# Attention and a feed-forward block on one core: weights' rounding with longer lags, second product started without sums of g, transposes in the score banks, first q and k loaded ahead of the branch

## Chip, core and metric

The kernel runs on one core of one Trainium2 chip. The metric is the device time of one execution in microseconds (us). TensorE is called PE here, its weight loads PEld, VectorE DVE, ScalarE ACT, GpSimd POOL; SP is SyncE, whose queue issues every DMA of this kernel.

## What is computed

```python
# q, k, v: (8, 12, 448, 64); g_q, g_k: (64,); w_in: (768, 2048); w_out: (2048, 768)
q_n, k_n = rmsnorm(q, g_q), rmsnorm(k, g_k)       # x / sqrt(mean(x*x) + 1e-6) * g
scores = q_n @ k_n.T / sqrt(64)
attn = softmax(scores)
x = (attn @ v) laid out as (8 * 448, 12 * 64)      # 3584 tokens, 768 columns
h = x @ w_in
out = relu(h) ** 2 @ w_out                         # (3584, 768)
```

q, k and v are float32; the two weights come as float64, and the kernel makes float32 of them from their 32-bit halves.

## The kernel before

**Spans and pairs.** A branch at the start (L928) picks the version whose scores need no row maximum; that is the one that runs. Its eight batches are four *spans* of two batches. A span has 12 attention *pairs* (two heads of one batch), then a first product (x by w_in) and a second product (g by w_out). Both products use a scheme with seven block products in place of eight: sums of quarters of x (xC, L642 to L654) and of g (gC, `combine`, L691 to L702) are the moving operands, sums of quarters of the weights the stationary ones. The seven sums of a weight block (A11, S2, S1, S3, A12, A22, S4) are made once, stored in DRAM (w1s, w2s) and loaded again in every span (`load_blocks`, L533, five buffers of tag sw).

**Rounding of the weights** (`prepare`, L438 to L510) is a generator of 35 *ticks* with four steps each; a tick t works on weight unit t and on the two or three units before it. Per unit: DVE takes the exponent out (L486), ACT bends it twice (L492, L493), DVE adds the sign (L471), cuts the mantissa (L476) and joins it (L477), ACT scales it (L483), POOL multiplies two halves (L459); for every second unit POOL makes four sums (L466) and SP stores the seven blocks (L499, L502). Loads of the raw words (L433, L436) go to one of five places (`place_of`), three of them towards the end. `EARLY`, `LATE` and `ALL` (L837) say how many steps are taken in which stage of span 0: 48 during its 12 attention pairs, 72 between its 56 first products, 20 between the two *alone* pairs that follow.

**Order.** There is no scheduler: the order on each engine is the program's. Span 0: 12 pairs alone, first product with rounding, two pairs of span 1 alone, `combine` for all of g (L871), then the second product of span 0 with the other ten pairs of span 1 threaded into it (L887 to L890). Spans 1 and 2: first product, then second product with the next span's 12 pairs (the *mixed* stage). Span 3: first and second product.

**A pair** (`attention`, L656): scores of key chunks 0 and 1 (L604, exponent on ACT at L607), `norm` of pair i+2 (ACT square, DVE reduction, POOL power L576 and two multiplications L578), in a mixed stage a stretch of second product, then the transposes of pair i+1 (L590; ACT copies them out at L596), scores of chunks 2 and 3, the values (L621), the sums of the exponents (L632), reciprocal and product on DVE (L638, L639). In `first_product` a helper `ahead` (L842) does the norms, loads and transposes of the next span's first pairs.

**PSUM.** Pool ps_s has two buffers of two banks (scores; pa of the first product), ps_o one bank each for values and sums, ps_m two single banks. ps_m serves pb, pc and pd, the accumulators ps of the second product, the two transposed tiles pt, and po, in which `deliver` (L776) turns a finished block for the output; ACT copies po out (L781). A tile waits until the one that held its buffer has been read.

The loop around the second product, which the change rewrites:

```python
for m in range(HC):                    # HC = 3
    for i in uses2:                    # A11, A12, S2, S1, S3, A22, S4
        ps = ps_m.tile(...)
        for c in range(HF): ...        # HF = 8 matmuls, a yield behind each
        ...                            # DVE adds; then, if a block is done, deliver() and a yield
```

Of the kernel before, what the change touches and what calls it, by code (L numbers as in the profile page):

```python
# [302 lines left out]

@with_exitstack
def attention_then_ffn_bounded(
# [9 lines left out]
    out: bass.AP,  # L315
):
# [28 lines left out]
    P = 128  # L345
# [22 lines left out]
    mhalf = consts.tile([SP, 2 * 2 * NJ], F32, name="mhalf")  # L368
    gT = consts.tile([P, NFC, 2 * S], F32, name="gT")
# [18 lines left out]
    WORDS, BLOCKS, LAST = 5, 3, 25  # L388
# [13 lines left out]
    def place_of(n):  # L402

        return n % WORDS if n < LAST else (0, 3, 4)[(n - LAST) % 3]
# [33 lines left out]
    def prepare(t):  # L438
# [24 lines left out]
        def total(n, dst, x, y, op):  # L463
            if there(n) and n % 2:
                b = parts(n)[0]
                nc.gpsimd.tensor_tensor(b[dst], b[x], b[y], op)  # L466

        if there(t - 1) and doubles:

            b, e, eu, low, f, high = parts(t - 1)  # L470
            nc.vector.scalar_tensor_tensor(eu, high, 0x80000000, eu, ALU.bitwise_and, ALU.bitwise_or)  # L471
        if there(t - 2):
            value(t - 2, 0)
        yield
        if there(t - 1) and doubles:
            nc.vector.tensor_scalar(high, high, 0xFFFFF, None, ALU.bitwise_and)  # L476
# [3 lines left out]
        total(t - 2, S1, A21, A22, ALU.add)  # L480
        yield
        if there(t - 1) and doubles:
            nc.scalar.activation(f, f, AF.Copy, bias=1.0, scale=2.0 ** -20)  # L483
        if there(t) and doubles:
            b, e, eu, low, f, high = parts(t)
            nc.vector.tensor_scalar(eu, high, 20, 0x7FF, ALU.logical_shift_right, ALU.bitwise_and)  # L486
        total(t - 2, S2, S1, A11, ALU.subtract)
        total(t - 2, S3, A11, A21, ALU.subtract)
        yield
        if there(t) and doubles:  # L490

            nc.scalar.activation(e, eu, AF.Relu, bias=clamp1, scale=-1.0)  # L492
            nc.scalar.activation(eu, e, AF.Relu, bias=clamp2, scale=-(2.0 ** 23))  # L493
        total(t - 2, S4, A12, S2, ALU.subtract)
# [34 lines left out]
    uses2 = (A11, A12, S2, S1, S3, A22, S4)  # L529
# [3 lines left out]
    def load_blocks(upto):  # L533

        while len(stream) < min(upto, NSPAN * (N1 + N2)):
# [7 lines left out]
            else:  # L543
                n -= N1
                src = w2s[n // (7 * (HF // 4)), uses2[n // (HF // 4) % 7], n % (HF // 4)]
# [7 lines left out]
    def load(i):  # L553
        b, h0 = i // NPAIR, 2 * (i % NPAIR)
        qk = loads.tile([SP, 2, 2, NJ * D], F32, tag="qk", name="qk")
        for dst, src in ((qk[:, 0], q), (qk[:, 1], k)):
            nc.sync.dma_start(dst, src[b, h0:h0 + 2].rearrange("h (p j) d -> p h (j d)", j=NJ))
        qks[i] = qk
# [26 lines left out]
    def transposes(i):  # L585
        qkn = normed.pop(i)
        pts[i] = [ps_m.tile([P, S], F32, tag="m", name="pt") for _ in range(2)]
# [10 lines left out]
    def scores(work, i, c, pe_sums):  # L598
# [7 lines left out]
        pr = work.tile([SP, 2, S], F32, tag="pr", name="pr", bufs=5)  # L606
# [49 lines left out]
    def attention(work, first, end, alone):  # L656
# [3 lines left out]
        for i in range(first, end):  # L660
# [12 lines left out]
            if i + 1 < last:  # L673
                transposes(i + 1)
                if not alone:
                    take_transposes(i + 1)
# [10 lines left out]
            if not alone:  # L687
                yield
# [77 lines left out]
    def second_product(work, span):  # L766
# [9 lines left out]
        def deliver(ct, col, t):  # L776
            pt = ps_m.tile([P, 512], F32, tag="m", name="po")
# [6 lines left out]
        for m in range(HC):  # L784
            for i in uses2:
                ps = ps_m.tile([P, S], F32, tag="m", name="ps")
                for c in range(HF):
                    load_blocks(n + 5)
                    nc.tensor.matmul(ps, stream[n][:, c % 4], rhs_of[i][:, c], start=c == 0, stop=c == HF - 1)  # L789
                    n += c % 4 == 3  # L790
                    if c < HF - 1:
                        yield
# [49 lines left out]
    def ahead(u, nxt):  # L842
# [4 lines left out]
        if u == 7 * (HF - 2):  # L847
            norm(nxt + 1)
# [114 lines left out]
```

## Time and profile before

| | us |
|---|---|
| median of 3 runs | 1643.68 (1640.68 to 1644.63) |
| the profiled execution, its own time | 1645.17 |
| its span, first to last instruction | 1643.4 |
| PE busy | 1515.0 (92%) |
| DVE, POOL, ACT busy | 727.7, 519.3, 484.7 |
| mean granted clock of PE, share of full speed | 0.977 |

The time of a run is the span and 1.8 us around it. "Busy" of PE counts the modelled length of overlapping matmuls; the distance from the start of one to the start of the next tells more, and stage lengths tell most. The kernel's float32 matmul is two instructions in the trace: 768 + 576 rows of ps are 672 matmuls of the program.

### The profile page before, as it was taken

To read this page: it belongs to the slowest core of one execution; us is meant where nothing else is said; L and a number is where in the kernel's file an instruction comes from. 1 tells how busy PE (TensorE), PEld (TensorE's weight loads), DVE (VectorE), ACT (ScalarE), POOL (GpSimd) and SP (SyncE) were. 2 spreads that over 40 slices of the span, in tenths; PEclk is the share of its full clock that TensorE was granted. 3 is DMA by queue.
4 is the path that set the end of the run, shared out by engine and by line. 5 is a ranking of instruction groups with operands and counts; after the bars stand their busy time and mean duration, and the time that the engine had idled before them with its cause. 6 is when DMAs were issued, how large, how long until landed. Compare 5 with 4: busy or idle time off the path is not lost.

```text
span 1643.4 us, 14375 instructions
## 1 busy us (share of the span) xinstructions
PE 1515.0 (92%) x5160; PEld 710.4 (43%) x5160; DVE 727.7 (44%) x849; ACT 484.7 (29%) x669; POOL 519.3 (32%) x391
## 2 busy tenths in 40 slices
PE   6999897747999999999999999989999999999998
PEld 2433443313444445444444445544444445555544
DVE  3787766456444422335445442334445551332001
ACT  4775554522232202113333311113332221111000
POOL 4795678652222002333223101242222200221000
PEclk9999998878999999999999999999999999999999
DMA  4565774641323232232332323223322223223332
GB/s 150 176 192 186 263 270 155 202 146 55 96 78 97 72 92 87 74 104 80 97 96 81 92 67 94 87 83 98 88 83 85 72 62 94 88 87 92 103 105 63
DMA packets 157716, 180.36 MB, mean 110 GB/s; under 512 B 10692, under 2 KB 134084, under 8 KB 157636
## 3 DMA queue, kind: packets, MB, share of 16 engines
q1 hardware_dynamic: 157636, 179.35, 36.3%
q8 instruction: 43, 0.70, 0.2%
q14 instruction: 37, 0.30, 0.1%
HBM read 146.28 MB, written 33.03 MB: 109 GB/s over the span
## 4 chain that ended last, share of the span: by engine, by line
PE 77%; DVE 7%; POOL 6%; ACT 4%; issue 4%; DMA 2%; SPq 1%; POOLq 0%; DVEq 0%; ACTq 0%
PE ps L789 31%; PE sc L604 9%; PE pav L621 7%; PE pd L713 7%; PE pc L713 7%; PE pa L713 6%; PE tot L632 4%; PE pb L713 3%; PE pt L590 2%; POOL gC L459 2%; POOL gC L466 1%; POOL rstd L576 1%; DVE acc L612 1%; ACT qkT L596 1%; POOL qkn L578 1%
## 5 line engine op out<-in xcount | busy, mean ns | idle before, releaser
L789 PE MATMUL ps<-gT,sw 128*128 128x448 f32 x768 | 310.9, 553 | 20.3 <-DMA sw<-w2s 10.8
L576 POOL TENSOR_TENSOR rstd<-rstd,mhalf 112x16 f32<-112x16 f32 x48 | 150.0, 3126 | 443.7 <-DVE rstd L575 420.6
L721 POOL TENSOR_TENSOR gT<-gT 128x448 f32<-128x448 f32 x112 | 112.7, 1007 | 519.6 <-ACT gT L717 519.6
L607 ACT ACTIVATE pr<-sc 112x896 f32<-112x896 f32 x192 | 166.0, 914 | 260.2 <-PE sc L604 260.1
L789 PE MATMUL ps<-gC,sw 128*128 128x448 f32 x576 | 230.1, 546 | 4.1 <-ACT osb L781 2.7
L789 PEld LDWEIGHTS ps<-gT,sw 128*128 128x128 f32 x768 | 142.7, 192 | 173.2 <-issue 143.8
L604 PE MATMUL sc<-qkT 64*112 64x448 f32 x768 | 175.7, 577 | 12.7 <-ACT pr L607 12.0
L638 DVE RECIPROCAL rec<-tot 128x448 f32<-128x448 f32 x48 | 142.0, 2958 | 78.2 <-PE tot L632 78.1
L621 PE MATMUL pav<-pr,vt 112*64 112x448 f32 x768 | 163.7, 550 | 3.4 <-DVE xT L639 3.4
L789 PEld LDWEIGHTS ps<-gC,sw 128*128 128x128 f32 x576 | 106.2, 190 | 118.0 <-issue 111.0
L713 PE MATMUL pa<-xT,sw 128*128 128x448 f32 x384 | 154.9, 539 | 0.0
L717 ACT ACTIVATE gT<-gT 128x448 f32<-128x448 f32 x96 | 55.3, 576 | 316.7 <-DVE gT L747 189.0
L612 DVE TENSOR_TENSOR acc<-acc,pr 112x896 f32<-112x896 f32 x68 | 78.8, 1159 | 140.7 <-ACT pr L607 137.1
L578 POOL TENSOR_TENSOR qkn<-qk,rstd 112x512 f32<-112x512 f32 x96 | 104.8, 1113 | 3.8
L781 ACT COPY osb<-po 112x512 f32<-112x512 f32 x48 | 28.2, 587 | 257.2 <-PE po L779 257.1
L713 PEld LDWEIGHTS pa<-xT,sw 128*128 128x128 f32 x384 | 72.9, 191 | 71.1 <-issue 71.1
L604 PEld LDWEIGHTS sc<-qkT 64*112 64x112 f32 x768 | 62.6, 177 | 93.6 <-issue 64.5
L596 ACT ACTIVATE qkT<-pt,gains 128x448 f32<-128x448 f32 x96 | 58.8, 636 | 131.7 <-PE pt L590 131.7
L621 PEld LDWEIGHTS pav<-pr,vt 112*64 112x64 f32 x768 | 51.2, 138 | 104.7 <-issue 80.1
L612 DVE TENSOR_TENSOR acc<-pr 112x896 f32<-112x896 f32 x34 | 37.1, 1092 | 131.5 <-ACT pr L607 131.5
L713 PE MATMUL pd<-xT,sw 128*128 128x448 f32 x192 | 81.7, 564 | 12.9 <-DVE z L736 12.9
L713 PE MATMUL pd<-xC,sw 128*128 128x448 f32 x192 | 82.5, 568 | 11.6 <-DMA sw<-w1s 11.1
(78 smaller groups left out, 1516.4 us busy)
## 6 DMA issues: line engine op xcount, KB each, us to landing
sw<-w1s SPq DMA_DIRECT2D x224, 192.0 KB, 2.4
sw<-w2s SPq DMA_DIRECT2D x168, 256.0 KB, 2.7
qk<-in_q_dram SPq DMA_DIRECT2D x48, 224.0 KB, 3.2
qk<-in_k_dram SPq DMA_DIRECT2D x48, 224.0 KB, 3.6
vt<-in_v_dram SPq DMA_DIRECT2D x48, 224.0 KB, 3.1
w1s<-gC SPq DMA_DIRECT2D x8, 1344.0 KB, 5.8
w2s<-gC SPq DMA_DIRECT2D x24, 448.0 KB, 4.4
out_dram<-osb SPq DMA_DIRECT2D x48, 224.0 KB, 2.9
```

The lines of the kernel that those rows point to most:

```text
L576: nc.gpsimd.tensor_tensor(rflat, rflat, mhalf, ALU.pow)
L578: nc.gpsimd.tensor_tensor(qkn[:, s].rearrange("p j h d -> p h j d"), qk[:, s].rearrange("p h (j d) -> p h j d", d=D), rstd[:, s].rearrange ...
L596: nc.scalar.activation(qkTs[i][:, s], pt, AF.Copy, scale=gains[:, s:s + 1])
L604: nc.tensor.matmul(sc[:, h, 0:S], qkT[rows, 1, c * SP:(c + 1) * SP], qkT[rows, 0, :], start=True, stop=True)
L607: nc.scalar.activation(pr, sc[:, :, 0:S], AF.Exp)
L612: nc.vector.tensor_tensor(accs[i], probs[i, 0] if c == 1 else accs[i], pr, ALU.add)
L621: nc.tensor.matmul(pavs[i][h * D:(h + 1) * D, :], vs[i][:, h, c, :], pr[:, h, :], start=(c == 0), stop=(c == NJ - 1))
L632: nc.tensor.matmul(tots[i][h * D:(h + 1) * D, :], ones, pr[:, h, :], start=first, stop=last)
L638: nc.vector.reciprocal(rec, tots.pop(i))
L713: nc.tensor.matmul(ps, stream[n][:, c], rhs[:, c], start=first and c == 0, stop=c == HC - 1, skip_group_check=not first)
L721: nc.gpsimd.tensor_tensor(g, g, g, ALU.mult)
L789: nc.tensor.matmul(ps, stream[n][:, c % 4], rhs_of[i][:, c], start=c == 0, stop=c == HF - 1)
```

## The change

- Load of the first pair's q and k (`load_pair`) and a small Exp on ACT stand ahead of the branch. q and k have two fixed buffers, qk0 and qk1.
- The rounding's steps are put in another order with longer lags: each consumer on another engine stands a step or more later, the four sums a tick later; from tick 12 on, S1 and S3 are made on DVE. There are six places for raw words (four towards the end), `LATE` is 33 ticks in place of 30: 84 steps in the first product, 8 in the alone pairs. pr has four buffers in place of five.
- The second product takes A11 and A12 of all three m first, which need no sum of g; in span 0 `combine` is spread over the first eight of the 21 products. `deliver` comes in the middle of the following product, and po is in ps_s.
- In mixed stages and in `ahead`, transposes are in ps_s (one tile for both); in mixed stages they come behind the sums of the exponents.
- `ahead` loads pair nxt+2 seven products later.

```diff
-    WORDS, BLOCKS, LAST = 5, 3, 25
+    WORDS, BLOCKS, LAST = 6, 3, 24
+    EARLY, LATE, ALL = 4 * 12, 4 * 33, 4 * (2 * NFC + 3)
...
+        late = t >= EARLY // 4
+        if there(t) and doubles:
+            nc.vector.tensor_scalar(eu, high, 20, 0x7FF, ALU.logical_shift_right, ALU.bitwise_and)
+        if there(t - 2) and doubles:
+            nc.scalar.activation(f, f, AF.Copy, bias=1.0, scale=2.0 ** -20)
+        total(t - 3, S1, A21, A22, ALU.add, late)
+        total(t - 3, S2, S1, A11, ALU.subtract)
+        yield
+            nc.scalar.activation(e, eu, AF.Relu, bias=clamp1, scale=-1.0)
+            nc.scalar.activation(eu, e, AF.Relu, bias=clamp2, scale=-(2.0 ** 23))
+        total(t - 3, S3, A11, A21, ALU.subtract, late)
+        total(t - 3, S4, A12, S2, ALU.subtract)
+        yield
...
-    uses2 = (A11, A12, S2, S1, S3, A22, S4)
+    uses2 = [(m, i) for m in range(HC) for i in (A11, A12)]
+    uses2 += [(m, i) for m in range(HC) for i in (S2, S1, S3, A22, S4)]
...
+            pt = ps_s.tile([P, 2, 512], F32, tag="s", name="pts")
+            pts[i] = [pt[:, s, 0:S] for s in range(2)]
...
-            pt = ps_m.tile([P, 512], F32, tag="m", name="po")
+            pt = ps_s.tile([P, 2, 512], F32, tag="s", name="po")[:, 0]
...
+                if c == HF // 2 - 1 and done:
+                    yield
                     deliver(*done.pop())
...
+            if span == 0 and j < 8:
+                for f in range(j % 4 * HF // 4, (j % 4 + 1) * HF // 4):
+                    combine(f, (j // 4,))
...
         if u == 7 * (HF - 3):
             norm(nxt)
-            load(nxt + 2)
         if u == 7 * (HF - 2):
             norm(nxt + 1)
+            load(nxt + 2)
...
-    for f in range(HF):
-        combine(f)
```

PE in a mixed stage, before: the transposes (pt, L590) stand between two stretches of second product and scores, and po (L779) between two products.

```order
L604 MATMUL sc<-qkT 112x448 x4
L789 MATMUL ps<-gC,sw 128x448 x6
L779 MATMUL po<-ident,ct 112x128 x4
L590 MATMUL pt<-ident,qkn 128x112 x8
L604 MATMUL sc<-qkT 112x448 x4
L621 MATMUL pav<-pr,vt 64x448 x8
L632 MATMUL tot<-acc,ones 64x448 x2
L789 MATMUL ps<-gC,sw 128x448 x8
```

PE in a mixed stage, now (L607 is the transposes, L621 the scores, L638 the values, L649 the sums, L809 the second product, L797 po):

```order
L621 MATMUL sc<-qkT 112x448 x4
L809 MATMUL ps<-gC,sw 128x448 x4
L809 MATMUL ps<-gT,sw 128x448 x4
L621 MATMUL sc<-qkT 112x448 x4
L638 MATMUL pav<-pr,vt 64x448 x8
L649 MATMUL tot<-acc,ones 64x448 x2
L607 MATMUL pts<-ident,qkn 128x112 x8
L797 MATMUL po<-ident,ct 112x128 x4
L809 MATMUL ps<-gT,sw 128x448 x4
L809 MATMUL ps<-gC,sw 128x448 x3
```

The transposes moved behind the sums, and po stands inside a product; what they wait for is now a score buffer and not the bank of ps.

DVE in the first product of span 0, before: one f, from its z (L736) to the next one's.

```order
L736 TENSOR_TENSOR z<-p_1364,pb 128x448
L471 SCALAR_TENSOR_TENSOR gC<-words,gC 128x768
L741 TENSOR_TENSOR y<-z,pc 128x448
L476 TENSOR_SCALAR words<-words 128x768
L477 SCALAR_TENSOR_TENSOR words<-words 128x768
L747 TENSOR_TENSOR gT<-y,pd 128x448
L486 TENSOR_SCALAR gC<-words 128x768
L471 SCALAR_TENSOR_TENSOR gC<-words,gC 128x768
L754 TENSOR_TENSOR gT<-z,pd 128x448
```

DVE there, now (L754 is z, L759 y, L765 and L772 two of g's blocks; L483 the exponent, L501 the sign, L502 and L507 the mantissa, L478 the sums S1 and S3):

```order
L754 TENSOR_TENSOR z<-p_1279,pb 128x448
L501 SCALAR_TENSOR_TENSOR gC<-words,gC 128x768
L502 TENSOR_SCALAR words<-words 128x768
L507 SCALAR_TENSOR_TENSOR words<-words 128x768
L759 TENSOR_TENSOR y<-z,pc 128x448
L483 TENSOR_SCALAR gC<-words 128x768
L478 TENSOR_TENSOR gC<-gC 128x384
L765 TENSOR_TENSOR gT<-y,pd 128x448
L478 TENSOR_TENSOR gC<-gC 128x384
L501 SCALAR_TENSOR_TENSOR gC<-words,gC 128x768
L502 TENSOR_SCALAR words<-words 128x768
```

Two sums per two units came in, and one exponent-to-sign distance grew: before, the sign (L471) follows the exponent (L486) at once in DVE's row; now the mantissa of the unit before and two or three other instructions, among them S1 and S3, stand in between.

## Rows read from the trace of the kernel before

**Rows 1.** Busy time by stretch: start:end, length, PE, PEld, DVE, ACT, POOL, PEclk, DMA share, GB/s.
```profile
151.38:312.37 160.99, 137.36 (x347) 66.98 (x345) 105.81 (x119) 79.23 (x113) 113.55 (x90) 0.94 0.68 223
312.37:388.41 76.04, 43.15 (x172) 16.61 (x171) 47.24 (x59) 26.12 (x33) 36.57 (x28) 0.78 0.38 118
606.64:739.99 133.35, 129.10 (x346) 65.00 (x345) 42.45 (x71) 25.44 (x44) 40.34 (x37) 0.99 0.32 92
739.99:988.52 248.53, 237.14 (x905) 107.19 (x905) 119.11 (x118) 72.81 (x95) 54.21 (x32) 1.00 0.29 84
1372.57:1498.85 126.28, 126.28 (x338) 63.84 (x337) 39.86 (x67) 22.46 (x40) 30.19 (x31) 1.00 0.32 93
```

**Rows 2.** Timeline of PE, alone pairs of span 0: start, length, instruction.
```profile
30.11 0.92 PE L621 MATMUL pav<-pr,vt 112*64 112x448 f32 x4
30.86 0.92 PE L632 MATMUL tot<-pr,ones 112*64 112x448 f32 x4
31.72 1.76 PE L604 MATMUL sc<-qkT 64*112 64x448 f32 x8
33.41 0.98 PE L590 MATMUL pt<-ident,qkn 112*128 112x112 f32 x8
...
42.18 1.76 PE L604 MATMUL sc<-qkT 64*112 64x448 f32 x8
```

**Rows 3.** Timeline of PE, mixed stage of span 1; in brackets the idle time and its releaser.
```profile
840.11 0.60 PE L779 MATMUL po<-ident,ct 128*112 128x128 f32 x4
841.01 2.52 PE L789 MATMUL ps<-gT,sw 128*128 128x448 f32 x6 [0.30 <-ACT p L795]
843.37 0.55 PE L590 MATMUL pt<-ident,qkn 112*128 112x112 f32 x4
844.74 0.57 PE L590 MATMUL pt<-ident,qkn 112*128 112x112 f32 x4 [0.82 <-ACT qkT L596]
```

**Rows 4.** PE's waits from 388 us to the end: us in total, times, longest.
```profile
PE pt L590 <- ACT qkT L596: 17.1, 21, 0.8
PE pd L713 <- DMA sw<-w1s: 8.2, 2, 4.4
```

**Rows 5.** SP's waits, 680 to 704 us.
```profile
SPq L557 <- POOL qkn L578: 6.7, 1, 6.7
```

**Rows 6.** PE's waits in the first product of span 0 (157 to 320 us).
```profile
PE pd L713 <- DVE z L736: 12.9, 5, 5.2
PE pb L713 <- ACT qkT L596: 7.0, 1, 7.0
```

**Rows 7.** DVE's waits, 150 to 365 us.
```profile
DVE gC L471 <- ACT gC L493: 29.7, 14, 3.3
```

**Rows 8.** Groups of instructions, 151.38 to 312.37 us: count, busy, mean ns, idle before.
```profile
L736 DVE TENSOR_TENSOR z<-p,pb 128x448 f32<-128x448 f32 x8 | 4.9, 614 | 7.5 <-PE pb L713 7.4
L466 POOL TENSOR_TENSOR gC<-gC 128x384 f32<-128x384 f32 x33 | 40.0, 1229 | 1.2
```

**Rows 9.** Groups of instructions, whole span: the sums of x on DVE.
```profile
L653 DVE TENSOR_TENSOR xC<-xT,xC 128x448 f32<-128x448 f32 x12 | 8.9, 741 | 0.4
```

**Rows 10.** DMA issues: count, KB each, median us to landing.
```profile
gT<-in_moe_w_in_dram SPq DMA_DIRECT2D x6, 768.0 KB, 7.6
```

**Rows 11.** Timeline, end of the rounding: last sums, last stores, second product.
```profile
353.08 3.99 POOL L466 TENSOR_TENSOR gC<-gC 128x384 f32<-128x384 f32 x4
...
357.10 1.71 SPq L502 DMA_DIRECT2D w2s<-gC  x3
...
365.32 7.46 PE L789 MATMUL ps<-gT,sw 128*128 128x448 f32 x14 [10.79 <-DMA sw<-w2s]
...
386.71 1.76 PE L632 MATMUL tot<-acc,ones 112*64 112x448 f32 x4 [7.31 <-DVE acc L612]
```

**Rows 12.** Timeline, start: second pair's square, then its transposes on PE.
```profile
12.54 1.06 ACT L571 ACTIVATE qkn<-qk 112x1024 f32<-112x1024 f32 x1 [2.58 <-DMA qk<-in_k_dram]
...
21.59 1.75 PE L590 MATMUL pt<-ident,qkn 112*128 112x112 f32 x8
```

More of the change, by code (lines that the diff above doesn't have):

```diff
@@ L315, in attention_then_ffn_bounded @@
     out: bass.AP,
+    qk0,
 ):
@@ L479, in prepare @@
             value(t - 2, 1)
[L480 to L494, printed above, removed]
         n = t - 3
@@ L553, in load @@
     def load(i):
[L554 to L558, printed above, removed]
+        qks[i] = (qk0, qk1)[i % 2]
+        load_pair(nc, qks[i], q, k, i)
     def load_v(i):
@@ L583, in norm, with transposes @@
         normed[i] = qkn
-    def transposes(i):
+    def transposes(i, alone=False):
         qkn = normed.pop(i)
-        pts[i] = [ps_m.tile([P, S], F32, tag="m", name="pt") for _ in range(2)]
+        if alone:
+            pts[i] = [ps_m.tile([P, S], F32, tag="m", name="pt") for _ in range(2)]
+        else:
+            pt = ps_s.tile([P, 2, 512], F32, tag="s", name="pts")
+            pts[i] = [pt[:, s, 0:S] for s in range(2)]
         for s, pt in enumerate(pts[i]):
@@ L605, in scores @@
                              start=True, stop=True)
-        pr = work.tile([SP, 2, S], F32, tag="pr", name="pr", bufs=5)
+        pr = work.tile([SP, 2, S], F32, tag="pr", name="pr", bufs=4)
         nc.scalar.activation(pr, sc[:, :, 0:S], AF.Exp)
@@ L672, in attention @@
                 load_v(i + 1)
[L673 to L676, printed above, removed]
+            if alone and i + 1 < last:
+                transposes(i + 1, True)
             scores(work, i, 2, alone)
@@ L687, in attention @@
             if not alone:
+                if i + 1 < last:
+                    transposes(i + 1)
+                    take_transposes(i + 1)
                 yield
@@ L782, in deliver @@
             nc.sync.dma_start(rows[2 * span + t, :, :, col * P:(col + 1) * P], osb)
[L784 to L792, printed above, removed]
-                if i == A11:
-                    p1 = work.tile([P, S], F32, tag="p1", name="p1", bufs=1)
-                    nc.scalar.copy(p1, ps)
-                elif i == S2:
-                    add(p1, p1, ps, ALU.add)
-                elif i == S1:
-                    y = work.tile([P, S], F32, tag="y", name="y", bufs=1)
-                    add(y, p1, ps, ALU.add)
-                else:
-                    ct = work.tile([P, S], F32, tag="ct", name="ct")
-                    add(ct, p1 if i in (A12, A22) else y, ps, ALU.add)
-                    if i == S3:
-                        add(p1, p1, ps, ALU.add)
-                yield
-                if done:
+        p1s, c11s = {}, {}
@@ L818, in second_product @@
         deliver(*done.pop())
         yield
-    load(0)
+    qks[0] = qk0
     for i, g in enumerate((g_q, g_k)):
@@ L858, in attention_then_ffn_bounded @@
         norm(1)
-        transposes(0)
+        transposes(0, True)
         take_transposes(0)
@@ L918 @@
     top = bound.tile([1, 1], F32, name="top")
+    qk0 = bound.tile([q.shape[2] // 4, 2, 2, 4 * D], F32, name="qk0")
+    load_pair(nc, qk0, q, k, 0)
     for i, g in enumerate((g_q, g_k)):
         nc.sync.dma_start(gg[:, i, :], g.rearrange("(o d) -> o d", o=1))
+    nc.vector.memset(top, 0.0)
+    nc.scalar.activation(top, top, AF.Exp)
     nc.vector.tensor_tensor(gg[:, 0, :], gg[:, 0, :], gg[:, 1, :], ALU.mult)
```

55 lines of the change are left out of this document (39 added, 16 removed).

## Prediction

> **What bounds the kernel now.** I read the busy time by stretch first, with the stretches cut where PE's lines change. The first product of span 3 runs undisturbed: 336 instructions, PE busy all of its 126.28 us [rows 1]. The same work in span 0 took 160.99 us, in span 1 133.35 us, with one set of eight transposes more (0.98 us, [rows 2]). So 33.7 and 6.1 us were lost there, though PE counts as 85% and 97% busy. Then I priced the other stages. A pair alone takes 10.46 us (31.72 to 42.18, [rows 2]); in a mixed stage it has four sum matmuls in place of 16, each four 0.75 us (30.11 to 30.86), so 8.21 us. The mixed stage beside span 1 should take 126.28 + 12 x 8.21 + 11 deliveries of four transposes (0.49 each) - 0.98 (one set of transposes stands in the stage before) = 229.2 us; it took 248.53 [rows 1], 19.3 us more. The stretch from 312.37 to 388.41 us holds two alone pairs, one mixed pair and 14 second-product instructions (5.23 us at 126.28 / 338): 34.4 us of work in 76.04 us, 41.7 lost. PE is the bound from 388 us on and loses time to small waits; before that it is span 0's rounding that holds it up. In both, the reader should look at the distance between stage length and priced work, not at PE's busy share.
>
> The forecast is made against the profiled execution's own 1645.17 us; the median of the runs is 1.5 us lower, which I take off at the end.
>
> **Part by part.**
>
> *PSUM banks (transposes and po in ps_s, po half a product later).* In a mixed stage one ps_m bank holds ps, so both transposed tiles go through the other: the second four transposes start 1.37 us behind the first, in place of 0.49, because they wait 0.82 us for ACT's copy [rows 3]; this came 21 times after 388 us [rows 4]. That is 0.88 x 11 = 9.7 us a stage. A delivery holds the bank that the next ps wants: 841.01 - 840.11 = 0.90 us in place of 0.49 [rows 3], 0.41 x 11 = 4.5 us. The other 5.1 of the 19.3 are waits of ps and pt for adds on DVE, of the same two banks. Afterwards ps alone alternates in ps_m and a bank is free for a whole product before its next use. The score buffers get the tenants instead: per pair four scores, one pts, about one po. The pts comes behind the sums, where the score tile two places back was read by ACT long ago, and the next scores come a stretch of product later; po beside scores can wait for one exponent (0.3 us or so by ACT's 0.9 us against PE's 0.9 us for a score tile; an estimate), and for its ct, which DVE now has half a product to make. I leave 3.3 us a stage for those: gain 16 + 16, and 14 for the ten pairs beside span 0. Span 3 has 12 deliveries: 5. Together **51**, bounds 35 (new waits of a half us per pair) and 61 (none).
>
> *`ahead`'s load seven products later.* Today the load of q and k behind the first norm holds SP for 6.7 us until POOL has multiplied [rows 5], and behind it stand loads of sw: PE waits 8.2 us in two waits, one per span [rows 4]. Afterwards that norm is two products old when SP comes to the load. Gain 6.1 in each of spans 1 and 2: **12**, bounds 8 and 14.
>
> *First product of span 0.* PE waited 12.9 us for z and 7.0 for ACT's copy of the transposes [rows 6]; the second goes outright, pts being in ps_s. z came late because DVE, in order, stood 29.7 us before the sign, for ACT's second bend [rows 7], and z, y and the g blocks queue behind. With the sign two steps later that wait should go. But three ticks more are put into this stage, and S1 and S3 for about 11 units. DVE's work now: 105.81 us less 40 adds at 0.614 [rows 8], less 8 for norms and the tail of the last pair, over 18 ticks: 4.07 us a tick. Then: 21 x 4.07 + 22 x 0.74 (the nearest DVE sum of two SBUF tensors under POOL's load, [rows 9]; 448 columns where these have 384) + 24.6 + 3 = 129 us. PE needs 127.3. Two engines of equal load, coupled with about one product of slack, won't both run through; I add 16 us for DVE's waits on products and on raw words. Stage 145: gain **15**. Bounds: 130 (gain 31) and today's pace, 160.99 / 18 x 21 = 188 (27 lost). I take the upper part since the wait that sets today's pace is the one removed. POOL loses 22 sums of 1.229 us [rows 8], so it is no bound.
>
> What the move of S1 and S3 costs is weighed once more. In the trace the comparable sum takes 0.741 us on the mean, so POOL at work delays it only by a part of its own length. The Trainium skill (SBUF — State Buffer, section on the two separate sides) says that a DVE instruction with two SBUF inputs and a GpSimd instruction take a shared port pair as an exclusive lock and that the loser waits for the other's whole length. By it these 22 sums would each wait for up to a whole POOL sum; that is the third rival. The row's 0.741 does not show it.
>
> *End of the rounding.* Today S4 is done at 357.07, the second product starts at 365.32, 8.2 us later (stores and first sw load), and then stands again 7.3 us, for acc, which queues on DVE behind `combine` [rows 11]. Now two ticks remain for the two alone pairs. The last S2 and S4 stand on POOL behind the norm that pair 13 issues: its scores and exponents 2.8 us, square to transposes 9.0 [rows 12] less a wait of about 0.9 there, two sums of 1.23, then 8.2: PE starts A11 about 21.6 us into pair 13, in place of 10.46 + 1.8 us. 9.3 lost; 2.8 for the first alone pair's exponents behind a late g (seen today too), 2 for half a clock after the wait (1.2 GHz; today this stretch has 0.78 of 2.4 on the mean, [rows 1]), 2 for `combine` beside attention: 16 lost in place of 41.7. Gain **26**, bounds 16 and 34.
>
> *Start and first attention.* The early load brings the first pair forward, but PE's first late wait is the second pair's transposes at 21.59, and their chain begins with a load landing at 12.54 [rows 12] that stays behind gains and v on SP; the branch itself now has two 224 KB loads ahead of g's. **0.5**, bounds -2 and 3. The eleven following pairs take 119.66 us to 151.38 against 115.06; shorter ACT waits give back **2** of these 4.6, bounds -2 and 4. pr with four buffers costs nothing: the values that free one stand ahead of the scores that want it. p1 in three buffers and the order of uses2 change no count of instructions.
>
> Sum: 51 + 12 + 15 + 26 + 2.5 = 106.5; 1645.2 - 106.5 - 1.5 = 1537, say 1538.
>
> **Rivals.**
> 1. *Rounding keeps its pace* (DVE waits for raw words, or ACT, as long as now): first product 188 us, 42 worse than forecast: 1580. For: one tick is now only 2.67 products, 6 us, and a load takes 7.6 us [rows 10]; it is issued a tick and more ahead. Against: rows 7.
> 2. *PE runs through:* stage 130, new waits nil: 1512. For: DVE's 129 us would fit just so.
> 3. *Sums block each other on DVE and POOL:* 22 x 1.23 = 27 us more on DVE, 129 + 27 + some waits = 161, no gain there: 1554. This is the page's rule above.
> 4. *Score banks crowd:* 32 pairs x 0.9 us of waits for score buffers, 29 back: 1567. Against: pts comes at the quiet end of the pair.
> 5. *Slower:* a ring in the first product: a load stands on SP behind a store that waits for S4 on POOL, POOL behind squares that wait for g on DVE, and DVE before the exponent that waits for this load. A tick is then landing, two values and two sums, 7.6 + 4 x 1.23 = 12.5 us, 21 of them 263 us, 102 over today; less the other 91.5: 1655. It decides from 12 us a tick on. Against: today the loads come ahead of DVE with one tick and a half, and no such wait is in the rows.
>
> **Chances.** Forecast (1520 to 1556 in itself) 0.60; rival 1 0.10; 2 0.12; 3 0.12; 4 0.04; 5 0.02. 1510 to 1574 leaves out rivals 1 and 5 and some tails, under 2 in 10. A measurement tells 0.3% (5 us) from no change: faster 0.97, same 0.01, slower 0.02.
>
> **What would show it.** Mixed stages of about 232 us, no waits of pt or ps for ACT; first products of spans 1 and 2 as long as span 3's; first product of span 0 about 145 us with DVE near 90% busy; from its end to the second product's first instruction 35 us. I am wrong if scores wait for ACT in mixed stages, if DVE waits for words or POOL in span 0, or if the mixed stages stay above 240 us.

## The result and the profile after

The changed kernel takes 1562.53 us (1561.18 to 1564.72, 4 runs) against 1642.18 (1638.71 to 1644.63, 4 runs): a ratio of 0.9518, 95% interval 0.9494 to 0.9541. The forecast was 1538. The profiled execution took 1561.18 us, 83.99 less than that of before, where the sum had 106.5. The page after, its span and its busy times:

```profile
span 1559.4 us, 14358 instructions
PE 1492.1 (96%) x5160; PEld 700.9 (45%) x5160; DVE 764.0 (49%) x874; ACT 481.0 (31%) x670; POOL 514.6 (33%) x367
```

Busy time by stretch, cut where PE's lines change; the row from 310.30 is the stretch between the first product of span 0 and the second product's first instruction (columns as in [rows 1]):

```profile
12.63:156.87 144.24, 133.55 (x673) 54.22 (x673) 103.03 (x99) 94.03 (x117) 107.46 (x70) 0.99 0.59 175
...
156.87:310.30 153.43, 138.43 (x346) 66.69 (x346) 128.47 (x149) 84.68 (x118) 107.52 (x82) 0.94 0.76 254
310.30:344.20 33.90, 22.80 (x122) 9.06 (x121) 22.45 (x23) 15.93 (x21) 26.25 (x18) 0.92 0.53 167
344.20:562.60 218.40, 216.96 (x808) 99.42 (x809) 115.16 (x125) 57.57 (x77) 36.42 (x21) 0.99 0.30 89
562.60:689.80 127.20, 127.20 (x348) 64.43 (x346) 42.45 (x71) 25.54 (x44) 40.32 (x37) 1.00 0.32 94
689.80:928.40 238.60, 233.84 (x905) 105.23 (x905) 125.77 (x118) 71.80 (x95) 59.99 (x32) 1.00 0.31 89
1294.20:1420.50 126.30, 126.30 (x338) 63.87 (x337) 39.85 (x67) 22.46 (x40) 30.15 (x31) 1.00 0.32 92
```

The two executions side by side (stage lengths in us, from the starts of PE's instructions):

| stage | before | after |
|---|---|---|
| to PE's first instruction | 15.69 | 12.63 |
| first attention | 135.69 | 144.24 |
| first product, span 0 | 160.99 | 153.43 |
| to the second product's first instruction | 52.95 | 33.9 |
| second product of span 0 with ten pairs | 241.3 | 218.4 |
| first products, spans 1 and 2 | 133.35, 135.6 | 127.2, 127.2 |
| mixed stages | 248.53, 248.5 | 238.6, 238.6 |
| first product, span 3 | 126.28 | 126.30 |
| rest | 144.55 | 138.9 |

First products of spans 1 and 2 now run through like span 3's. The mixed stages and the first product of span 0 gained less than forecast, and the first attention took 8.5 us longer; as it began 3.1 us earlier, it ended 5.5 us later. PE's waits from 344 us to the end (us in total, times, longest; the first stands ahead of the second product of span 0):

```profile
PE ps L809 <- DMA sw<-w2s: 10.4, 1, 10.4
PE tot L649 <- DVE acc L629: 7.5, 14, 0.9
PE po L797 <- DVE ct L826: 3.4, 5, 0.8
```

No wait of transposes (pts) or ps for ACT is left of [rows 4], and none for a score buffer came in. Three views of the trace after show where time was lost. Waits of the first attention, of SP's queue and of PE:

```profile
SPq L514 <- POOL gC L478: 51.3, 4, 16.4
```

```profile
PE pt L607 <- POOL qkn L591: 19.0, 8, 12.6
PE pav L638 <- DMA vt<-in_v_dram: 2.7, 2, 1.7
```

L514 is the store of a weight block. It stands in the same tick as the four sums that it needs; the 48 steps come four at once, behind a pair, so SP reaches the store before POOL has made the sums. In the kernel before, with the last sums of a unit a tick earlier, the same stores waited:

```profile
SPq L499 <- POOL gC L466: 22.1, 4, 6.4
```

Behind the store stand the loads of q, k and v. (The 12.6 is the wait ahead of the first pair, which the kernel before has too.)

Groups of the mixed stage beside span 1 (mean ns of one), and the timeline of a pair there, POOL and DVE one instruction at a time:

```profile
L629 DVE TENSOR_TENSOR acc<-acc,pr 112x896 f32<-112x896 f32 x24 | 34.9, 1455 | 31.2 <-ACT pr L624 29.6 <-DVE acc L629 0.5
L591 POOL TENSOR_TENSOR qkn<-qk,rstd 112x512 f32<-112x512 f32 x20 | 28.8, 1462 | 0.8
L629 DVE TENSOR_TENSOR acc<-pr 112x896 f32<-112x896 f32 x12 | 13.1, 1092 | 43.7 <-ACT pr L624 43.7
```

```profile
753.52 1.04 POOL L591 TENSOR_TENSOR qkn<-qk,rstd 112x512 f32<-112x512 f32 x1
753.62 1.89 DVE L629 TENSOR_TENSOR acc<-acc,pr 112x896 f32<-112x896 f32 x1 [3.16 <-ACT pr L624]
754.52 1.89 POOL L591 TENSOR_TENSOR qkn<-qk,rstd 112x512 f32<-112x512 f32 x1
755.61 1.74 DVE L629 TENSOR_TENSOR acc<-acc,pr 112x896 f32<-112x896 f32 x1
...
757.41 0.97 PE L649 MATMUL tot<-acc,ones 112*64 112x448 f32 x4 [0.88 <-DVE acc L629]
```

The sums of exponents (acc) fall on the moment of POOL's multiplications (qkn): 1455 ns against 1092 for the first sum, which stands elsewhere, and PE stands 0.88 us before the sum matmuls (in this stage 3.7 us in seven waits).

PE's waits in the first product of span 0, and the group of the moved sums on DVE there:

```profile
PE pc L731 <- DMA sw<-w1s: 5.8, 3, 3.4
PE pd L731 <- DVE z L754: 4.1, 3, 3.0
PE pb L731 <- DMA sw<-w1s: 1.3, 1, 1.3
```

```profile
L478 DVE TENSOR_TENSOR gC<-gC 128x384 f32<-128x384 f32 x21 | 15.7, 762 | 8.8 <-POOL gC L471 8.8
```

Against [rows 6] the wait for ACT's copy (7.0) is gone and z fell from 12.9 to 4.1, but waits for block loads (sw) grew from 2.9 us to 8.8. sw is loaded on SP, whose queue there also holds loads of raw words (L448) and stores (L517) that wait for POOL and DVE:

```profile
SPq L448 <- POOL gC L471: 25.4, 7, 9.3
SPq L517 <- DVE gC L478: 18.0, 6, 8.7
```

### The profile page after: what moved, and what is told of

Its sections match the earlier page's. It is cut to its first block, busy times and chain, and to the rows that moved or that the text cites. A ratio compares the mean times of both kernels' runs of the same rounds, so it can differ in the third digit from the quotient of the medians.

```text
span 1559.4 us, 14358 instructions
## 1 busy us (share of the span) xinstructions
PE 1492.1 (96%) x5160; PEld 700.9 (45%) x5160; DVE 764.0 (49%) x874; ACT 481.0 (31%) x670; POOL 514.6 (33%) x367
## 4 chain that ended last, share of the span: by engine, by line
PE 79%; POOL 7%; DVE 5%; DMA 4%; issue 3%; ACT 2%; SPq 1%; POOLq 0%; DVEq 0%; ACTq 0%
PE ps L809 33%; PE sc L621 8%; PE pc L731 8%; PE pd L731 8%; PE pa L731 7%; PE pav L638 4%; DVE acc L629 4%; PE pb L731 4%; PE tot L649 3%; PE pts L607 2%; POOL rstd L589 2%; POOL gC L471 2%; ACT pr L624 2%; DMA sw<-w1s 2%; PE po L797 1%
## 5 line engine op out<-in xcount | busy, mean ns | idle before, releaser
L809 PE MATMUL ps<-gT,sw 128*128 128x448 f32 x768 | 305.7, 545 | 10.4 <-DMA sw<-w2s 10.4
L809 PE MATMUL ps<-gC,sw 128*128 128x448 f32 x576 | 230.3, 543 | 0.0
L809 PEld LDWEIGHTS ps<-gT,sw 128*128 128x128 f32 x768 | 142.6, 191 | 146.5 <-issue 134.6
L621 PE MATMUL sc<-qkT 64*112 64x448 f32 x768 | 173.4, 571 | 1.9 <-ACT pr L624 1.0
L638 PE MATMUL pav<-pr,vt 112*64 112x448 f32 x768 | 162.5, 546 | 2.7 <-DMA vt<-in_v_dram 2.7
L809 PEld LDWEIGHTS ps<-gC,sw 128*128 128x128 f32 x576 | 105.5, 190 | 101.1 <-issue 99.0
L629 DVE TENSOR_TENSOR acc<-acc,pr 112x896 f32<-112x896 f32 x68 | 95.8, 1409 | 96.2 <-ACT pr L624 92.3
L591 POOL TENSOR_TENSOR qkn<-qk,rstd 112x512 f32<-112x512 f32 x96 | 117.5, 1245 | 3.8
L621 PEld LDWEIGHTS sc<-qkT 64*112 64x112 f32 x768 | 61.6, 175 | 96.6 <-issue 84.2
L638 PEld LDWEIGHTS pav<-pr,vt 112*64 112x64 f32 x768 | 51.4, 137 | 102.3 <-issue 85.1
L629 DVE TENSOR_TENSOR acc<-pr 112x896 f32<-112x896 f32 x34 | 37.1, 1092 | 119.5 <-ACT pr L624 119.5
L731 PE MATMUL pc<-xC,sw 128*128 128x448 f32 x192 | 81.6, 563 | 5.3 <-DMA sw<-w1s 5.3
L731 PE MATMUL pd<-xC,sw 128*128 128x448 f32 x192 | 77.8, 541 | 3.3 <-DVE gT L765 2.1
```

The lines of the kernel that those rows point to most:

```text
L591: nc.gpsimd.tensor_tensor(qkn[:, s].rearrange("p j h d -> p h j d"), qk[:, s].rearrange("p h (j d) -> p h j d", d=D), rstd[:, s].rearrange ...
L621: nc.tensor.matmul(sc[:, h, 0:S], qkT[rows, 1, c * SP:(c + 1) * SP], qkT[rows, 0, :], start=True, stop=True)
L629: nc.vector.tensor_tensor(accs[i], probs[i, 0] if c == 1 else accs[i], pr, ALU.add)
L638: nc.tensor.matmul(pavs[i][h * D:(h + 1) * D, :], vs[i][:, h, c, :], pr[:, h, :], start=(c == 0), stop=(c == NJ - 1))
L731: nc.tensor.matmul(ps, stream[n][:, c], rhs[:, c], start=first and c == 0, stop=c == HC - 1, skip_group_check=not first)
```

## Experiments

Every kernel is the changed one with the edit shown, timed in rounds with the kernel before. Ratios are to the kernel before.

**First attention: store_later.** Each store stands at the start of the next tick.

```diff
+        if there(t - 4) and t % 2:
+            store(t - 4)
...
-        if there(n) and n % 2:
+        if t == 2 * NFC + 2:
+            store(t - 3)
```

> The changed kernel, with each store of seven weight blocks issued at the start of the next tick instead of at the end of the tick that makes their sums (the last store stays). Theory: in the first attention of span 0, where a whole tick is issued at once per pair, SP stands before each store until POOL has made the sums (51.3 us in 4 waits in the changed kernel, 22.1 before), and the next pairs' q, k and v queue behind it; then the stretch from PE's first instruction to the first product falls from 144.2 us to about 136 and the total by 6 to 10 us; the SP waits for stores nearly go. Rival: POOL itself is late there (port contention with DVE, more waits for the reduction), the store only shows it; then the stretch stays within 2 us of 144 and so does the total.

1562.78 us, ratio 0.9525 (0.9505 to 0.9545): no gain in all, against the theory. But the first attention fell from 144.2 to 140.0, half of what the theory had, and the first product rose from 153.4 to 161.8. SP's wait for sums in the first attention, and DVE's in the first product:

```profile
SPq L483 <- POOL gC L478: 8.8, 3, 3.1
```

```profile
DVE gC L496 <- DMA w2s<-gC: 13.7, 3, 5.7
```

Three places for blocks are too few for a store that comes a tick later where ticks are short: the exponent (L496) writes into a block still being stored. So the store's place costs the first attention 4 us, and moving it pays only there.

**First attention: vector_sums_always.** S1 and S3 are on DVE there too.

```diff
-        late = t >= EARLY // 4
+        late = True
```

> Edit: S1 and S3 of the weight blocks are made on DVE from the first tick on, not from tick 12 on. Theory A (the first attention of the changed kernel, 144.2 us, is held by POOL, which has about 10 of a pair's 10.46 us of work there and which the stores on SP's queue and the norm's multiplications wait for): 2.4 us of sums per two ticks leave POOL, the wait of the transposes for the norm (19.0 us in 8) falls under 10 us, the first attention goes to 136 to 139 us, the whole to 1555 to 1559. Theory B (POOL is not what holds it; a store that stands behind its sums in the same tick blocks SP's queue wherever the sums are made): first attention 142 to 146, the whole within 3 us of 1562.5. The first product (153.4 us) should not move by more than 3 us under either.

1557.6 us, ratio 0.9473 (0.9457 to 0.9489). First attention 140.1, first product 156.8. The busy times of the first attention:

```profile
12.90:153.00 140.10, 131.29 (x672) 53.84 (x673) 102.84 (x106) 93.91 (x117) 100.32 (x62) 1.00 0.61 181
```

POOL has 7 us less (107.46 before the edit) and the stage is 4 us shorter: theory A, short of its numbers (136 to 139, and PE's 19.0 us of waits for the norm fell only to 16.1); the store still waits in its tick. The first product's 3.4 us more is not put down to the edit: kernels whose edit lies elsewhere had 153.7 (combine_first) to 156.5 (norm_first) in it, and 143.4 to 145.8 in the first attention.

**Start: load_behind.** The first q and k are loaded behind the branch.

```diff
-    qks[0] = qk0
+    load(0)
...
-    load_pair(nc, qk0, q, k, 0)
```

> The changed kernel with the first q and k loaded behind the branch, as before (the early Exp stays). Forecast's theory: the early load moves PE's first transposes by 3 us but the second pair's by only 1.6, so without it the total is 0 to 2 us longer. Rival: it is worth the whole 3 us.

1560.53 us, ratio 0.9512 (0.9496 to 0.9528), not to be told from the changed kernel. The timeline of PE, first of the changed kernel, then of this one:

```profile
12.63 1.92 PE L607 MATMUL pt<-ident,qkn 112*128 112x112 f32 x8 [12.63 <-POOL qkn L591]
15.50 3.33 PE L621 MATMUL sc<-qkT 64*112 64x448 f32 x8 [0.96 <-ACT qkT L613]
20.02 2.01 PE L607 MATMUL pt<-ident,qkn 112*128 112x112 f32 x8 [1.19 <-POOL qkn L591]
```

```profile
14.19 1.92 PE L607 MATMUL pt<-ident,qkn 112*128 112x112 f32 x8 [14.19 <-POOL qkn L591]
16.83 3.25 PE L621 MATMUL sc<-qkT 64*112 64x448 f32 x8 [0.72 <-ACT qkT L613]
20.01 1.01 PE L607 MATMUL pt<-ident,qkn 112*128 112x112 f32 x8
```

PE starts 1.56 us later and comes to the second pair's transposes at the same time: the early load is worth nothing. The first attention even ended at 155.1 us here, against 156.9 in the changed kernel; the first product, 2 us longer, gave that back.

**First product: sums_on_pool.** All four sums stay on POOL.

```diff
-        late = t >= EARLY // 4
+        late = False
```

> The changed kernel with S1 and S3 back on POOL in the first product. Theory: DVE, 128.0 us busy of 153.4 there, is what holds the stage; without 22 sums it falls to about 114 us busy and the stage to 146 to 150, unless POOL (107 us, then about 130) takes over; total 0 to 6 us faster. Rival: POOL is the one that the stores and loads wait for, and the move to DVE was worth its price; then the stage grows by 5 to 15 us.

1568.99 us, ratio 0.9559 (0.9543 to 0.9575). Its first product and PE's longest wait in it:

```profile
158.00:318.40 160.40, 136.93 (x344) 66.40 (x344) 116.97 (x129) 86.33 (x120) 129.10 (x102) 0.95 0.72 243
```

```profile
PE pc L731 <- DMA sw<-w1s: 13.4, 4, 5.3
```

160.4 against 153.4, the rival's 5 to 15: moving 22 sums to DVE gained 4 to 7 us, by the 153.4 to 156.5 that the changed kernel and those whose edit lies elsewhere had. With POOL at 129 us DVE's waits for raw words grew from 3.4 us to 14.1, and PE's for block loads with them.

**First product: late_30.** LATE is 30 ticks, as before: three ticks go from the first product to the alone pairs.

```diff
-    EARLY, LATE, ALL = 4 * 12, 4 * 33, 4 * (2 * NFC + 3)
+    EARLY, LATE, ALL = 4 * 12, 4 * 30, 4 * (2 * NFC + 3)
```

> Edit: LATE is 30 ticks in place of 33, so 18 ticks stand in span 0's first product and five in the alone pairs, as in the kernel before; the new order of the steps stays. Theory A (the rounding's pace, some 7.3 us a tick, is what sets the first product's length): the first product falls from 153.4 to 131 to 138, and the gap behind it grows from 33.9 by 15 to 20, the whole within 5 us of 1562.5. Theory B (PE's own small waits for z, g and block loads set it, whatever the number of ticks): first product 148 to 154, the gap 49 to 54, the whole 1574 to 1580.

1569.05 us, ratio 0.9549 (0.9533 to 0.9565). Between the theories:

```profile
158.60:301.75 143.15, 134.32 (x346) 65.71 (x346) 114.91 (x135) 77.68 (x110) 95.88 (x73) 0.96 0.76 252
```

DVE has 13.6 us less than in the 153.43 us of the changed kernel, and the stage is 10.3 shorter; the stretch behind it grew by 15.8. So three ticks cost 10 us in the first product, 16 behind it.

**The rounding whole: old_rounding.** The order of steps, lags, five places, LATE of 30 and all sums on POOL as before the change (the removed lines of `prepare` in the change's diff); the rest new.

```diff
-    WORDS, BLOCKS, LAST = 6, 3, 24
+    WORDS, BLOCKS, LAST = 5, 3, 25
-    EARLY, LATE, ALL = 4 * 12, 4 * 33, 4 * (2 * NFC + 3)
+    EARLY, LATE, ALL = 4 * 12, 4 * 30, 4 * (2 * NFC + 3)
```

> Edit: the rounding's order of steps, its lags, five places, LATE of 30 ticks and all sums on POOL as in the kernel before; banks, second product, early load and four buffers of pr as in the changed kernel. Theory A (longer lags and sums on DVE are what shortened span 0's first product, and cost the first attention): first attention back to 135 to 138 us, first product up from 153.4 to 158 to 162 (it was 161.0, of it 7.0 a wait for the transposed tile's bank that stays away), from its end to the second product's first instruction up from 33.9 to 43 to 53: in all 1570 to 1578. Theory B (the gain in span 0 comes from combine leaving the way and from the banks, not from the rounding): first product 152 to 155, the gap 33 to 38, the whole 1550 to 1558, so faster than the changed kernel. The mixed stages stay at 238.6 under both.

1574.43 us, ratio 0.9582 (0.9566 to 0.9598), as theory A has it in all, but the gain lies elsewhere: first attention 139.5, first product 152.1 (theory B's 152 to 155), the stretch behind it 53.8. DVE's longest wait there is the old one of [rows 7], ACT's second bend before the sign:

```profile
152.00:304.10 152.10, 137.17 (x346) 66.88 (x344) 106.64 (x117) 78.14 (x111) 113.10 (x89) 0.94 0.70 232
```

```profile
DVE gC L483 <- ACT gC L505: 26.8, 14, 3.3
```

At the same 18 ticks late_30 takes 143.2: the order, lags and moved sums are worth 9 us of first product. The change spends them on three ticks more: its first product is as long as with the old rounding, and the stretch behind it 20 us shorter. The kernel before, with the same old rounding, took 161.0 for the first product: so what this stage gained by the change (7.6) is not the rounding's.

**Mixed stages: norm_first.** The norm of pair i+2 stands ahead of scores 0 and 1.

```diff
+            if not alone and i + 2 < last:
+                norm(i + 2)
             scores(work, i, 0, alone)
             scores(work, i, 1, alone)
-            if i + 2 < last:
+            if alone and i + 2 < last:
                 norm(i + 2)
```

> The changed kernel, with the norm of pair i+2 issued ahead of the scores of chunks 0 and 1 in mixed stages, not behind them. Theory: with the transposes gone from between the scores, the two sums of exponents on DVE now run while POOL multiplies q and k (3.73 us for two in place of 2.29), and PE waits for acc (7.5 us in 14 waits); an earlier norm ends on POOL before them, each mixed stage falls from 238.6 us by 3 to 4.5, the total by 8 to 12 us, and the acc sums are back at 1.1 us. Rival: PE waits for acc because the scores of chunks 2 and 3 come back to back with the values, whatever POOL does; then the waits stay and the total is within 2 us; if the earlier square delays the exponents, scores wait and it is slower by 1 to 5 us.

1548.21 us, ratio 0.9435 (0.9419 to 0.9450). Mixed stages 232.7 each, which is the theory with a larger gain than its 3 to 4.5 us a stage. The groups that answer to those above, and two sums beside an idle POOL:

```profile
L629 DVE TENSOR_TENSOR acc<-acc,pr 112x896 f32<-112x896 f32 x24 | 26.2, 1092 | 37.1 <-ACT pr L624 35.9
L591 POOL TENSOR_TENSOR qkn<-qk,rstd 112x512 f32<-112x512 f32 x20 | 24.8, 1262 | 0.8
L629 DVE TENSOR_TENSOR acc<-pr 112x896 f32<-112x896 f32 x12 | 14.3, 1192 | 24.1 <-ACT pr L624 24.1
```

```profile
753.06 2.29 DVE L629 TENSOR_TENSOR acc<-acc,pr 112x896 f32<-112x896 f32 x2 [4.50 <-ACT pr L624]
```

The late sums are back at 1092 ns and the wait of the sum matmuls is gone; the multiplications now meet the first sum (1192), for which nobody waits. The edit is worth 5.9 us of each mixed stage: 3.7 are PE's seven waits for acc, 2 a shorter busy time of PE (233.84 to 231.89). That all of it was this meeting is likely, but ACT's and DVE's part of the norm moved as well.

**Mixed stages: banks_back.** The transposed tiles and po go back to ps_m, at the new places in the program.

```diff
-        if alone:
+        if True:
             pts[i] = [ps_m.tile([P, S], F32, tag="m", name="pt") for _ in range(2)]
...
-            pt = ps_s.tile([P, 2, 512], F32, tag="s", name="po")[:, 0]
+            pt = ps_m.tile([P, 512], F32, tag="m", name="po")
```

> Edit: the transposed tiles are two tiles of ps_m again and po is in ps_m, each at the place in the program that it has in the changed kernel. Theory A (the pool of banks is what the mixed stages gained by): each mixed stage loses the 9.7 us of the second transposes' wait and about 4 of po's, so 238.6 becomes 248 to 252; the ten pairs beside span 0 lose 8 to 12, the first products of spans 1 and 2 go from 127.2 to 130 to 134; in all 1590 to 1605. Theory B (the place in the program, half a product later for po and behind the sums for the transposes, is what counts): mixed stages within 3 us of 238.6, the whole 1560 to 1570.

1606.24 us, ratio 0.9779 (0.9763 to 0.9796): theory A, and taking the banks back costs 43.7 us. Mixed stages 253.1 and 254.6, longer than before the change; the second product of span 0 227.4; first products of spans 1 and 2 127.9, less than theory A's 130 to 134. The mixed stage, and PE's wait in it:

```profile
702.40:955.50 253.10, 238.38 (x906) 106.27 (x906) 125.76 (x118) 73.05 (x95) 59.97 (x32) 0.99 0.28 84
```

```profile
PE pt L607 <- ACT qkT L613: 8.2, 10, 0.8
```

The wait of [rows 4] is back. In the old banks the new places, with acc meeting POOL, cost 4.6 and 6.1 us a stage against the kernel before (253.1 and 254.6 against 248.5), so these 10.7 of the 43.7 are no part of the gain. The first product of span 0 rose to 158.1, with the wait of [rows 6] for ACT's copy:

```profile
PE pb L731 <- ACT qkT L613: 5.8, 1, 5.8
```

**Mixed stages: pts_early.** The transposes stand ahead of scores 2 and 3 again, in a score buffer.

```diff
-            if alone and i + 1 < last:
-                transposes(i + 1, True)
+            if i + 1 < last:
+                transposes(i + 1, alone)
+                if not alone:
+                    take_transposes(i + 1)
             scores(work, i, 2, alone)
...
-                if i + 1 < last:
-                    transposes(i + 1)
-                    take_transposes(i + 1)
```

> Edit: in mixed stages the transposes of pair i+1 stand ahead of the scores of chunks 2 and 3 again, in a score buffer. Theory A (their place behind the sums is needed, since ahead of two score tiles they make the scores wait for ACT's copy): 0.4 to 0.9 us a pair, so each mixed stage goes from 238.6 to 243 to 250 and the whole to 1578 to 1592. Theory B (with a score buffer of their own turn the place doesn't matter): mixed stages within 2 us of 238.6, the whole 1559 to 1567. Earlier transposes can also take PE off the scores while acc waits; then a mixed stage would be 1 to 3 us shorter.

1568.46 us, ratio 0.9543 (0.9527 to 0.9559). Mixed stages 240.2, 1.6 longer and so within theory B; the second product of span 0 221.8, 3.4 longer. PE waits where theory A put it, but for less:

```profile
PE sc L621 <- ACT qkT L613: 3.4, 11, 0.3
```

The 1.6 us are what is left of two effects: PE's wait for acc fell from 3.7 us to 0.2, as the scores and with them acc come later and off POOL's multiplications (median of the late sums 1093 ns). Against norm_first's 232.7, where acc is off them too, the earlier place is 7.5 us longer a stage, as theory A has it; no run has both edits.

**End of the rounding: combine_first.** All of `combine` stands ahead of the second product.

```diff
-            if span == 0 and j < 8:
-                for f in range(j % 4 * HF // 4, (j % 4 + 1) * HF // 4):
-                    combine(f, (j // 4,))
...
+    for f in range(HF):
+        combine(f)
     for span in range(NSPAN):
```

> Edit: combine for all of g stands ahead of the second product of span 0 again, as in the kernel before; the order of the 21 products stays the new one. Theory A (spreading it is worth the 7.3 us that PE stood behind acc in the kernel before): from the second product's first instruction to the first product of span 1 218.4 us becomes 224 to 228, nothing else moves, the whole 1568 to 1573. Theory B (the 32 sums fit into DVE's idle time while PE waits for the last weights, so that spreading them is worth nothing): that stretch within 2 us of 218.4, the whole 1560 to 1565.

1570.24 us, ratio 0.9563 (0.9546 to 0.9579). The stretch from the second product's first instruction to the next first product rose from 218.4 to 228.8, as theory A has it, and the wait of [rows 11] for acc is back (the one for sw is in the changed kernel too):

```profile
PE ps L809 <- DMA sw<-w2s: 8.9, 1, 8.9
PE tot L649 <- DVE acc L629: 7.6, 1, 7.6
```

**A better version: norm_first_store_12, then best_sums.** norm_first, load_behind, and the store a tick later while the tick is under 12; in best_sums the sums of vector_sums_always as well.

```diff
+        if there(t - 4) and t % 2 and t < EARLY // 4:
+            store(t - 4)
...
-        if there(n) and n % 2:
+        if there(t - 3) and t % 2 == 0 and t >= EARLY // 4:
+            store(t - 3)
...
-        late = t >= EARLY // 4
+        late = True
```

> Edit: the norm of pair i+2 ahead of the first scores in mixed stages (1548.2 us alone), each store of a weight block at the start of the next tick while the tick is under 12, the first q and k loaded behind the branch. Theory A (the store behind its own sums holds up the first attention, and only there is moving it free): first attention 139 to 141 us, first product 153 to 157, mixed stages 232.7, the whole 1541 to 1545. Theory B (as with every store moved, what the first attention gains the first product gives back, because the rounding as a whole is the bound of both): first attention 139 to 141 but first product 159 to 163, the whole 1547 to 1550.

> Edit: the version with the norm ahead of the scores in mixed stages, stores a tick later while the tick is under 12 and the first load behind the branch (1540.2 us), and S1 and S3 on DVE from the first tick on. Theory A (POOL still holds its first attention, 135.4 us): first attention 131 to 134, first product 155 to 157, the whole 1536 to 1539. Theory B (with the store moved POOL is no bound there any more, and DVE comes late instead): first attention 135 to 139, the whole 1540 to 1545.

1540.16 us (1540.10 to 1540.35), ratio 0.9374 (0.9359 to 0.9390), and 1536.73 us (1536.47 to 1536.94), ratio 0.9350 (0.9335 to 0.9366). These intervals overlap; both lie clear of the changed kernel's. In the first of them the first attention is 135.4, shorter than either theory had it, and the first product 155.4: what one gains the other does not give back. The busy times of best_sums, first attention and first product:

```profile
14.30:145.60 131.30, 129.38 (x672) 52.59 (x672) 101.22 (x106) 92.68 (x116) 99.21 (x62) 1.00 0.62 191
145.60:299.70 154.10, 135.41 (x346) 65.28 (x344) 129.78 (x150) 84.73 (x118) 108.09 (x82) 0.97 0.74 250
```

PE is busy for 129.38 of 131.30 us. Theory A of both runs holds, though the first attention of the first and the first product of the second (154.1) came out below its numbers. Of the 12.9 us that the first attention of best_sums is shorter than the changed kernel's, 1.7 are its later start.

## Why the prediction was right and wrong

| term | forecast | measured |
|---|---|---|
| PSUM banks | 51 | 38 |
| `ahead`'s load | 12 | 14.5 |
| first product of span 0 | 15 | 7.6 |
| end of the rounding | 26 | 29.5 |
| start, first attention | 2.5 | -5.5 |
| sum | 106.5 | 84.1 |

Measured: the banks are 9.9 twice, 12.5 of the second product of span 0 (22.9 less the 10.4 that combine_first took back) and 5.65 in the rest. `ahead` is what spans 1 and 2 gained in their first products, of which banks_back took 0.7 each; no run puts its load back alone, but the two waits of [rows 4] for sw are gone. The end is 19.1 and those 10.4. The first product's 7.6 is 4.5 to 7.6 by the kernels whose edit lies elsewhere.

The measured 1562.5 us lies in 1510 to 1574, but above the 1520 to 1556 that the forecast had in itself. It is nearest to rival 4's 1567 by chance: no view shows that rival's waits for score buffers.

*Banks.* The mechanism was right: no transposes or ps wait for ACT any more, and banks_back puts the loss back. "Gain 16" a stage was mis-sized: it measured 9.9. The step that failed is the list of what would be late next. I named scores and ct; it was mostly acc (7.5 us of waits, ct 3.4), whose two late sums the new place of the work put beside POOL's multiplications. With that undone the stage is 232.7, "about 232". The Trainium skill (SBUF — State Buffer, section "SBUF: two separate sides") says that a DVE instruction with two SBUF inputs and a GpSimd instruction that reads SBUF share a port pair: whichever starts first holds it for its whole length, and the other is blocked. In the timeline above, the first multiplication has its usual 1.04 us. Each later instruction is lengthened (by 0.80, 0.85 and 0.65; a sum alone takes 1.09) by nearly what the other engine's instruction still had to run when it began (0.94, 0.99 and 0.80). In all, both engines were done 3.83 us after the start; strictly in turns it would be 4.33 (two sums alone 2.29, two multiplications alone 2.04), and with no meeting 2.39. So the trace agrees with the rule nearly, in a place where I had not looked for it.

*First product.* DVE's work was forecast well in all: 129 us, measured 128.47. But that a moved sum, put at 0.741 us, took 0.762 is luck. I read the 0.741 of [rows 9] as the length of a sum under POOL's load; it is a mean that hides two lengths, and so is the 0.762 (ns, shortest/median/longest; first the kernel before, then the changed one):

```profile
L653 DVE TENSOR_TENSOR xC<-xT,xC x12: 624/626/1328, 134.6 to 1353.5; 128x448 f32<-128x448 f32 x12
L478 DVE TENSOR_TENSOR gC<-gC x21: 542/558/1291, 162.5 to 309.6; 128x384 f32<-128x384 f32 x21
```

Ten of the twelve met no POOL instruction and took 624 to 626 ns; the two that began while POOL added or multiplied took 1306 and 1328. Of the moved sums, the eight that began so took 1036 to 1291, the other thirteen 542 to 559. So "POOL at work delays it only by a part of its own length" was a wrong reading: the row that I held against the third rival bears its mechanism out. Its size is wrong: the meetings cost DVE some 4.4 us in this stage, not 27, since most sums began beside no such instruction, and sums_on_pool shows that the move was a gain.

"16 us for DVE's waits" was mis-sized: the stage is 25 above DVE's work. The terms that it named, products and raw words, measured 7.2 and 3.4 us; two waits that it put at nothing came to more:

```profile
DVE gC L478 <- POOL gC L471: 8.8, 4, 3.0
DVE rstd L587 <- ACT qkn L584: 4.3, 2, 2.9
```

The first is a moved sum that waits for the values that POOL makes; DVE's wait for POOL was one of the forecast's own signs of being wrong. On PE's side, 15 us of the stage are idle, part of them for block loads on SP's queue, which for this stage I had named only in the fifth rival. Another 11 are longer busy time: 138.43 us at a mean granted clock of 0.94, where span 1's first product has 127.20 at 1.00. The forecast took 127.3 for PE. In 256.58 to 264.25 us, behind a stretch with PE busy for 4.75 of 7.67 us, the granted clock was 0.56 on the mean, so mostly the lower of its two levels (1.2 of 2.4 GHz): 11 instructions kept PE busy for 6.97 us, and at 1.00, in 202.89 to 210.56, 22 fill 7.67.

What the stage did gain is the banks' part: the 7.0 us for ACT's copy went "outright", as forecast, and banks_back brings 5.8 of them back. The longer lags, worth 9 us (old_rounding against late_30), were spent on three more ticks.

*First attention.* "Shorter ACT waits give back 2" failed outright. I followed the waits on the engines and not SP's: sums and store now stand in one tick, and four steps are issued at once. With the old order of steps (old_rounding) the first attention ends at 152.0 us, in the kernel before at 151.4, in the changed one at 156.9. store_later (-4.2), vector_sums_always (-4.1) and best_sums (131.3 in place of 144.2, 1.7 of it its later start) show store and POOL as the cause. Of the early load I had written that the second pair's chain comes first; load_behind bears that out.

*End of the rounding.* Right within its bounds, by both of its parts. The forecast of 35 us for the stretch measured 33.9. old_rounding shows its price: three more ticks in the first product, which eat what the new lags gain there.

No run takes away any of the 25 us between DVE's work and the first product's length, so what they are worth one by one stays open; loads of raw words on another queue would tell of a part.

## What to carry to other kernels

When a step moves, list which engines' work it will now coincide with, not only which buffers it frees: here the freed banks were worth 16 us a stage, and 6 of them went to two engines whose instructions met. Before a group's mean is used as a price, look at its shortest and longest: a mean of 741 ns was ten sums of 625 and two of twice that. A DMA issue belongs behind its producer by as much as the queue behind it can't afford to wait, and stages of different pace want different distances. Where one stretch of work is stretched over two stages, price a unit in each of them: a tick cost 3.4 us in the first product and 5.3 behind it.

## What was unexpected of the hardware

The same sum on DVE took 1092 ns beside an idle POOL and 1455 ns on the mean where it met POOL's multiplications, and those took 1462 ns on the mean where one alone takes about 1040. No wait shows this: the instructions themselves are longer, by nearly what the other engine's had still to run. In the first product of span 0, where POOL was busy for 107.52 of 153.43 us, thirteen of 21 moved sums took about 550 ns and eight about twice as long. How much is lost hangs on which instruction begins while which other runs; neither POOL's busy share nor a group's mean tells it.
